# Four attention units on unscaled keys, a fixed order for VectorE's first steps, and eight query tiles

## The chip, the cores and the metric

The program runs on one core of a Trainium2 chip. Its engines are TensorE (PE; PEld is its weight load), VectorE (DVE), ScalarE (ACT), GpSimd (POOL) and SyncE (SP); SP and ACT issue the transfers. The metric is the time of one execution in device microseconds (us), the median of several runs.

## The reference

An attention whose queries see a window of 31 keys and 24 block summaries, then two feed-forward layers. All is float32.

```python
k_sum = k.reshape(B, H, nb, block, D).max(axis=3)      # B 2, H 8, S 768, D 64, block 32
v_sum = v.reshape(B, H, nb, block, D).mean(axis=3)
scores_l = scale * (q @ k.T); mask_l = abs(i - j) < 16
scores_s = scale * (q @ k_sum.T) + log(block)
a = exp(scores_all - max(scores_all)); a = a / (sum(a) + 1e-9)
x = a @ concat([v, v_sum])                             # 1536 tokens x 512
h = x @ w_in;  x = (h * sigmoid(1.702 * h)) @ w_out    # width 2048
out = (sigmoid(x @ w_gate) * (x @ w_val)) @ w_out2     # width 1536
```

## The kernel before, in words

**Attention.** The work is cut into 24 units (b, g, hp): two batches, three groups of four query blocks of 64, four pairs of heads. Units 0 to 11 are batch 0, units 12 to 23 batch 1. A unit needs its query tile (`load_q`, 256 KB) and the keys of its batch and head pair (`load_k`, one tile for three units). `prep_k` takes the block maxima of the keys on VectorE (L670). `w_copy` (L681) lets GpSimd put the windows of keys (128x384) and the maxima (128x128) together into one scaled tile `kx`. `b_pe` writes the mask into PSUM by a matmul with `pick` (L690) and adds four matmuls on `kx` (L692); the scores lie in one of three PSUM tiles `ps_s`. `b_max` (L697) takes the negated row maximum `nm`, `b_exp` (L705) four exponentials, `n_inv` the reciprocal of the sums, `n_mul` (L719, GpSimd) the division; `c_pe` (L725) transposes into `ps_p`, `c_copy` (L730) copies to `pt`, `d_pe` (L744) multiplies with the values, and `d_hi`, `d_lo` (L762, L765) split the result into a high and a low part, xH and xL. `sum_v` (L654) and `sum_lay` (L663, L664) make the block means of the values, `vs`, from the transposed values `vt`.

**Weights.** Each 1 MB piece is fetched by `fetch` (L218) and decoded by `load` in steps: clamp and shift on VectorE (L123), a Prelu on ScalarE (L131), a merge (L137), a cast (L140) and a difference (L142); this gives a high and a low half, so that a product takes three matmuls.

**Feed-forward.** `first` makes ps_h from xH, xL and a piece of w_in (24 matmuls of 512 columns for 512 tokens; the first batch of 512 tokens is made of units 0 to 7); a sigmoid (L501), a product (L485) and a split into gh (ScalarE, L493) and gl (GpSimd, L494) follow; `second` multiplies them with a piece of w_out into ps_o (24 matmuls). Four such steps (`filler`) run among the attention units, the rest behind them.

**Order.** The main loop is written unit by unit, but the order of the compute engines is chosen by a scheduler; SP keeps the order that is written. Every engine works its own list strictly in order, and a matmul that waits holds up all matmuls behind it. A query tile's place comes free when the unit that used it has its scores; before, there are five places. Weight pieces wait for one of two places, key tiles have five.

Of the kernel before, what the change touches and what calls it, by code (L numbers as in the profile page):

```python
# [29 lines left out]
def attention_moe_moe2_kernel(ctx: ExitStack, tc: tile.TileContext, ins: dict, out: bass.AP):  # L30
# [77 lines left out]

    def load(layer, g, i, early):
# [21 lines left out]
        nc.scalar.activation(af, af, AF.Prelu, scale=REBIAS, alpha=-2.0 ** 32)  # L131
# [456 lines left out]
    with tc.manual_schedule(engines={mybir.EngineType.SP}), ExitStack() as es:  # L588
        one = es.enter_context(tc.tile_pool(name="a_one", bufs=1))
        qp = es.enter_context(tc.tile_pool(name="a_q", bufs=5))  # L590
# [9 lines left out]
        pick = one.tile([P, P], BF16, name="pick")  # L600

# [48 lines left out]
        def sum_v(b, hp):  # L650
            if hp == 0:
                vpart[b] = vp.tile([P, HP, W0], F32, tag="vm", name=f"vm{b}")
                nc.vector.memset(vpart[b], 0.0)
            nc.vector.tensor_reduce(  # L654
                out=vpart[b][:, hp, 0:NB], in_=vtl.pop((b, hp)).rearrange("p (n t) -> p n t", t=BLK),
                axis=AX.X, op=ALU.add,
            )

        def sum_lay(b):
            r = vpart.pop(b)  # L660
            ps = ps_a.tile([W0, H * D], F32, tag="x", name="ps_v", bufs=2)
            for hp in range(HP):
                nc.tensor.matmul(ps[:, hp * P:(hp + 1) * P], lhsT=r[:, hp], rhs=ident, start=True, stop=True)  # L663
            nc.scalar.activation(vsum[b][0:W0], ps, AF.Copy, scale=1.0 / BLK)  # L664

        def prep_k(b, hp):
            ks = kp.tile([P, W0], F32, tag="ks", name=f"ks{b}_{hp}")
            nc.vector.memset(ks, 0.0)
            own = kraw[b, hp][:, HALO:HALO + S].rearrange("p (n t) -> p n t", t=BLK)
            nc.vector.tensor_reduce(out=ks[:, 0:NB], in_=own, axis=AX.X, op=ALU.max)  # L670
            kmax[b, hp] = ks

        def w_copy(u):

            b, g, hp = units[u]
            t = kxp.tile([P, G, P], F32, tag="kx", name=f"kx{u}")
            r = kraw[b, hp][:, g * G * QB:g * G * QB + P - W0]
            src = bass.AP(r.tensor, r.offset, [r.ap[0], [QB, G], [1, P - W0]])
            top = kmax[b, hp].unsqueeze(1).to_broadcast([P, G, W0])
            for to, x in ((t[:, :, W0:P], src), (t[:, :, 0:W0], top)):  # L680
                nc.gpsimd.tensor_scalar(out=to, in0=x, scalar1=scale, scalar2=None, op0=ALU.mult)  # L681
            kx[u] = t

        live = {}

        def b_pe(u):
            b, g, hp = units[u]
            t, kt = qbd.pop(u), kx.pop(u)
            ps = ps_a.tile([P, G, P], F32, tag="s", name="ps_s", bufs=3)
            nc.tensor.matmul(ps, lhsT=pick, rhs=mask[:, g:g + G, :], start=True, stop=False)  # L690
            for j in range(G):
                nc.tensor.matmul(ps[:, j, :], lhsT=t[:, j, :], rhs=kt[:, j, :], start=False, stop=j == G - 1)  # L692
            live["s", u] = ps

        def b_max(u):
            nm = sp.tile([P, G], F32, tag="nm", name="nm")
            nc.vector.tensor_reduce(out=nm, in_=live["s", u], axis=AX.X, op=ALU.max, negate=True)  # L697
            live["nm", u] = nm

        def b_exp(u):  # L700
            s, nm = live.pop(("s", u)), live.pop(("nm", u))
            sm = sp.tile([P, G], F32, tag="sm", name="sm")
            e = ep.tile([P, G, P], F32, tag="e", name="e")
            for j in range(G):
                nc.scalar.activation(  # L705
                    e[:, j, :], s[:, j, :], AF.Exp, bias=nm[:, j:j + 1], accum_out=sm[:, j:j + 1]
                )
            live["e", u], live["sum", u] = e, sm

        def n_inv(u):  # L710
            rs = sp.tile([P, G], F32, tag="rs", name="rs")
            nc.vector.tensor_scalar(out=rs, in0=live.pop(("sum", u)), scalar1=EPS, scalar2=None, op0=ALU.add)
            rr = sp.tile([P, G], F32, tag="rr", name="rr")
            nc.vector.reciprocal(out=rr, in_=rs)
# [119 lines left out]
        now = [0]  # L834
        fill = filler()
        for t in range(-1, NU + LD):
# [3 lines left out]
            if u < NU and units[u][1] == 0:  # L840
                prep_k(units[u][0], units[u][2])
            for part, lag in ORDER:
                if 0 <= t - lag < NU:
                    part(t - lag)
            if 0 <= t < NU - 5:
                load_q(t + 5, nc.sync)
            if t == -1:
                sum_v(0, 0)
                sum_v(0, 1)
            if t == 0:  # L850
                sum_v(0, 2)
                sum_v(0, 3)
                sum_lay(0)
                load_v(0, 1)
                put_v(0, 1, nc.scalar)
# [16 lines left out]
            if t >= 1:  # L872
                pull(1 if t < 6 or t > 9 else 2)
# [153 lines left out]
```

## Time and profile before

| | us |
|---|---|
| median of 3 runs | 618.84 (617.81 to 620.34) |
| the profiled execution | 619.4 |
| its span | 617.6 |
| TensorE busy in the span | 603.2 |
| VectorE, ScalarE, GpSimd busy | 465.9, 307.3, 212.7 |

What lies around the span is 1.8 us. A matmul of 128x512 starts every 0.227 us where TensorE runs without a gap, though each is listed with 0.39 us, since they overlap; so a stretch in which TensorE is busy is not always one in which it is full.

### The profile page before, as it was taken

How to read it: one execution, taken by the hardware profiler on the slowest of the kernel's cores; microseconds unless marked ns; L12 is line 12 of the kernel's file. 1: busy time of each engine (PE TensorE's matmuls, PEld its weight loads, DVE VectorE, ACT ScalarE, POOL GpSimd, SP SyncE). 2: the span in 40 equal slices, each digit the busy share in tenths (PEclk: the TensorE clock that was granted, in tenths of full speed). 3: DMA queues.
4: the chain of work that ended last, by engine and by line, in shares of the span. 5: the costliest groups of instructions: out<-in, count | busy, mean ns of one | idle time of the engine just before them, and what ended most of it. 6: DMA issues, size and time to landing. Idle time of an engine off the chain costs nothing.

```text
span 617.6 us, 8819 instructions
## 1 busy us (share of the span) xinstructions
PE 603.2 (98%) x3354; PEld 501.7 (81%) x3354; DVE 465.9 (75%) x684; ACT 307.3 (50%) x614; POOL 212.7 (34%) x168
## 2 busy tenths in 40 slices
PE   7798999999999999999999999999999999999997
PEld 4676777788878888888888898888898898898896
DVE  6699665389998778797769889577969768877434
ACT  4688657556443353435445566635335335444230
POOL 6797585323363423233231232022122021131030
PEclk9899999999999999999999999999999999999999
DMA  9998753034221104040102013321312222100014
GB/s 314 347 313 286 232 137 70 1 121 153 68 69 68 53 17 137 1 137 10 60 0 69 1 40 101 132 69 33 105 69 69 68 69 70 68 1 1 0 49 156
DMA packets 25161, 58.10 MB, mean 94 GB/s; under 512 B 1568, under 2 KB 1824, under 8 KB 25120
## 3 DMA queue, kind: packets, MB, share of 16 engines
q1 hardware_dynamic: 24400, 56.24, 28.0%
q10 hardware_dynamic: 720, 1.31, 0.6%
q8 instruction: 26, 0.43, 0.3%
q14 instruction: 15, 0.12, 0.1%
HBM read 53.08 MB, written 3.15 MB: 91 GB/s over the span
## 4 chain that ended last, share of the span: by engine, by line
PE 81%; DVE 8%; ACT 3%; issue 3%; DMA 2%; POOL 2%; SPq 0%; ACTq 0%; POOLq 0%; DVEq 0%
PE ps_o L474 32%; PE ps_y L178 15%; PE ps_x L178 10%; PE ps_v L178 10%; PE ps_h L474 5%; PE ps_h L178 4%; PE ps_s L692 2%; ACT e L705 1%; PE ps_x L744 1%; DMA raw<-in_moe_w_out 1%; POOL gl L494 1%; DMA vt<-in_vt 1%; PE ps_p L725 1%; DVE da L137 1%; DVE w_0L L142 1%
## 5 line engine op out<-in xcount | busy, mean ns | idle before, releaser
L494 POOL TENSOR_TENSOR gl<-sg,gh 128x512 fp32r<-128x512 f32 x84 | 125.9, 1505 | 362.1 <-ACT gh L493 256.2
L557 DVE TENSOR_TENSOR acc<-ps_o,acc 128x512 f32<-128x512 f32 x143 | 95.9, 683 | 46.7 <-PE ps_o L474 46.6
L474 PE MATMUL ps_o<-gl,w_1H 128*128 128x512 f32 x192 | 75.5, 394 | 0.5 <-POOL gl L494 0.5
L493 ACT CAST gh<-sg 128x512 fp32r<-128x512 f32 x84 | 51.5, 620 | 48.0 <-DVE sg L485 38.6
L474 PE MATMUL ps_o<-gh,w_1H 128*128 128x512 f32 x192 | 74.6, 390 | 0.0
L474 PE MATMUL ps_o<-gh,w_1L 128*128 128x512 f32 x192 | 72.1, 396 | 1.9 <-ACT gh L493 1.7
L474 PE MATMUL ps_o<-w_2L,gh 128*128 128x512 f32 (+1 forms) x146 | 56.6, 388 | 0.0
L474 PE MATMUL ps_o<-w_2H,gh 128*128 128x512 f32 (+1 forms) x146 | 56.2, 386 | 0.0
L474 PE MATMUL ps_o<-w_2H,gl 128*128 128x512 f32 (+1 forms) x146 | 56.2, 389 | 0.1
L137 DVE SCALAR_TENSOR_TENSOR da<-da,db 128x1024 uint32<-128x1024 uint32 x34 | 46.1, 1357 | 5.7 <-ACT da L131 5.1
L131 ACT ACTIVATE da<-da 128x1024 f32<-128x1024 f32 x34 | 36.1, 1061 | 24.7 <-DVE da L123 22.9
L474 PEld LDWEIGHTS ps_o<-gh,w_1L 128*128 128x128 f32 x192 | 35.9, 188 | 9.9 <-ACT gh L493 2.3
L474 PEld LDWEIGHTS ps_o<-gl,w_1H 128*128 128x128 f32 x192 | 36.0, 188 | 8.5 <-POOL gl L494 1.5
L474 PEld LDWEIGHTS ps_o<-gh,w_1H 128*128 128x128 f32 x192 | 36.1, 188 | 7.3
L705 ACT ACTIVATE e<-ps_s,nm 128x128 f32<-128x128 f32 x96 | 34.2, 377 | 9.6 <-DVE nm L697 7.1
L681 POOL TENSOR_SCALAR kx<-k 128x384 f32<-128x384 f32 x24 | 33.3, 1389 | 14.6 <-PE ps_s L692 7.5
L474 PE MATMUL ps_h<-xH,w_0L 128*128 128x512 f32 x96 | 37.7, 401 | 0.0
L474 PE MATMUL ps_h<-xL,w_0H 128*128 128x512 f32 x96 | 37.6, 392 | 0.0
L474 PE MATMUL ps_h<-xH,w_0H 128*128 128x512 f32 x96 | 37.5, 390 | 0.0
L485 DVE TENSOR_TENSOR sg<-ps_h,sg 128x512 f32<-128x512 f32 x32 | 21.7, 682 | 14.1 <-ACT sg L501 11.9
L474 PEld LDWEIGHTS ps_o<-w_2H,gh 128*128 128x128 f32 x146 | 27.4, 188 | 5.8
L474 PEld LDWEIGHTS ps_o<-w_2L,gh 128*128 128x128 f32 x146 | 27.5, 188 | 4.9
(242 smaller groups left out, 1504.5 us busy)
## 6 DMA issues: line engine op xcount, KB each, us to landing
raw<-in_moe_w_out SPq DMA_DIRECT2D x13, 1024.0 KB, 4.9
raw<-in_moe_w_in SPq DMA_DIRECT2D x8, 1024.0 KB, 7.0
raw<-in_moe_w_gate SPq DMA_DIRECT2D x6, 1024.0 KB, 5.1
raw<-in_moe_w_val SPq DMA_DIRECT2D x6, 1024.0 KB, 5.1
q<-in_q SPq DMA_DIRECT2D x20, 256.0 KB, 8.5
vwin<-in_v SPq DMA_DIRECT2D x6, 768.0 KB, 8.6
k<-in_k SPq DMA_DIRECT2D x8, 400.0 KB, 7.2
out<-acc SPq DMA_DIRECT2D x11, 256.0 KB, 2.0
```

The costliest lines, as they stand in the source:

```text
L131: nc.scalar.activation(af, af, AF.Prelu, scale=REBIAS, alpha=-2.0 ** 32)
L137: nc.vector.scalar_tensor_tensor(out=a, in0=a, scalar=3, in1=b, op0=ALU.logical_shift_left, op1=ALU.bitwise_or)
L142: nc.vector.tensor_tensor(out=lo.rearrange(flat), in0=af, in1=hi.rearrange(flat), op=ALU.subtract)
L178: nc.tensor.matmul(ps, lhsT=a[x][:, kk, :], rhs=b[y][:, kk, :], start=start and i == 0, stop=i == n - 1, skip_group_check=True,)
L474: nc.tensor.matmul(ps, lhsT=a, rhs=b, start=i == 0, stop=i == n - 1)
L485: nc.vector.tensor_tensor(out=sg, in0=val, in1=sg, op=ALU.mult)
L493: nc.scalar.copy(gh, sg)
L494: nc.gpsimd.tensor_tensor(out=gl, in0=sg, in1=gh, op=ALU.subtract)
L557: nc.vector.tensor_tensor(out=a[:, m, :], in0=ps, in1=a[:, m, :], op=ALU.add)
L681: nc.gpsimd.tensor_scalar(out=to, in0=x, scalar1=scale, scalar2=None, op0=ALU.mult)
L692: nc.tensor.matmul(ps[:, j, :], lhsT=t[:, j, :], rhs=kt[:, j, :], start=False, stop=j == G - 1)
L705: nc.scalar.activation(e[:, j, :], s[:, j, :], AF.Exp, bias=nm[:, j:j + 1], accum_out=sm[:, j:j + 1])
```

## The change

There are four parts. For units 0 to 3 (`DIRECT`) there is no `kx`: the four window products read the loaded keys (96 columns) and four more the block maxima (32 columns), with a mask scaled by 8 (`pick8`); the scale moves into the exponential, and `nm` gets a multiplication on ScalarE. VectorE's steps of the loop's first rounds (`in_turn`: block maxima, row maxima, sums, means) are tied to one another in the order that is written, with the means spread over rounds 0, 1, 3 and 4 and the last stage of a unit moved by a round. The first weight decode stands behind them. And the query tiles have eight places.

```diff
+    def behind(a, b):
+        tc.add_manual_dep(a.ins, b.ins.name, ... NoSync ..., reason="order")
...
+            elif (layer, g, i) == (1, 0, 0):
+                behind(ins, turn[-1])
...
+        ins = nc.scalar.activation(af, af, AF.Prelu, scale=REBIAS, alpha=-2.0 ** 32)
+        if (layer, g, i) == (1, 0, 0):
+            behind(ins, ahead["exp"])
...
-        qp = es.enter_context(tc.tile_pool(name="a_q", bufs=5))
+        QUERIES = 8
+        qp = es.enter_context(tc.tile_pool(name="a_q", bufs=QUERIES))
...
-            nc.vector.tensor_reduce(out=vpart[b][:, hp, 0:NB], ...)
+            in_turn(nc.vector.tensor_reduce(out=vpart[b][:, hp, 0:NB], ...))
...
+                if b == 0:
+                    behind(ins, live["last"])
...
         def w_copy(u):
+            if u < DIRECT:
+                return
...
+        def in_turn(ins):
+            if now[0] <= ORDERED:
+                if turn:
+                    behind(ins, turn[-1])
+                turn.append(ins)
+        now, ORDERED = [-1], 4
+        DIRECT = HP
...
+            if u < DIRECT:
+                nc.tensor.matmul(ps, lhsT=pick8, rhs=mask[:, g:g + G, :], start=True, stop=False)
+                for j in range(G):
+                    win = kraw[b, hp][:, (g * G + j) * QB:(g * G + j) * QB + P - W0]
+                    nc.tensor.matmul(ps[:, j, W0:P], lhsT=t[:, j, :], rhs=win, start=False, stop=False)
+                for j in range(G):
+                    nc.tensor.matmul(ps[:, j, 0:W0], lhsT=t[:, j, :], rhs=kmax[b, hp], start=False, stop=j == G - 1)
+                return
...
+            if u < DIRECT:
+                nc.scalar.mul(nm, nm, scale)
...
-                    e[:, j, :], s[:, j, :], AF.Exp, bias=nm[:, j:j + 1], accum_out=sm[:, j:j + 1]
+                    e[:, j, :], s[:, j, :], AF.Exp, bias=nm[:, j:j + 1],
+                    scale=scale if u < DIRECT else 1.0, accum_out=sm[:, j:j + 1],
...
         load_v(0, 0)
+        load_q(4, nc.sync)
         sum_load(0, 2)
         sum_load(0, 3)
-        load_q(4, nc.sync)
+        load_q(5, nc.sync)
+        load_q(6, nc.sync)
         fetch()
+        load_q(7, nc.sync)
...
+        nc.vector.tensor_scalar(out=pick8, in0=pick, scalar1=1.0 / scale, scalar2=None, op0=ALU.mult)
...
-            if 0 <= t < NU - 5:
-                load_q(t + 5, nc.sync)
-            if t == -1:
-                sum_v(0, 0)
-                sum_v(0, 1)
+                if part is b_max:
+                    if 0 < t < HP - 1:
+                        prep_k(0, t + 1)
+                    if t in (0, 1, 3, 4):
+                        sum_v(0, {0: 0, 1: 1, 3: 2, 4: 3}[t])
+                    if t == 4:
+                        sum_lay(0)
+                        put_v(0, 1, nc.scalar)
+            if 0 <= t < NU - QUERIES:
+                load_q(t + QUERIES, nc.sync)
             if t == 0:
-                sum_v(0, 2)
-                sum_v(0, 3)
-                sum_lay(0)
...
-            if t >= 1:
-                pull(1 if t < 6 or t > 9 else 2)
+            if t > ORDERED:
+                pull(1 if t > 9 else 2)
```

The first place is SP's list of transfers from the last key tile of batch 0 to the first of batch 1 (`k1_0`; `raw` and `xH1_0_1` are weight pieces of 1 MB, the number behind q is the unit). Before:

```order
L616 DMA q4_150<-in_q 128x512
L218 DMA raw1_0_0_152<-in_moe_w_in 128x4x512
L616 DMA q5_209<-in_q 128x512
...
L218 DMA xH1_0_1_221<-in_moe_w_out 128x2x1024
L616 DMA q6_248<-in_q 128x512
...
L616 DMA q13_584<-in_q 128x512
L218 DMA raw1_1_1_586<-in_moe_w_out 128x2x1024
L647 DMA vt1_1_588<-in_vt 128x768
L609 DMA k1_0_593<-in_k 128x800
```

And the same stretch of SP's list now:

```order
L631 DMA q4_148<-in_q 128x512
...
L631 DMA q6_155<-in_q 128x512
L231 DMA raw1_0_0_157<-in_moe_w_in 128x4x512
L631 DMA q7_159<-in_q 128x512
L631 DMA q8_212<-in_q 128x512
...
L231 DMA xH1_0_1_215<-in_moe_w_out 128x2x1024
...
L631 DMA q16_596<-in_q 128x512
L231 DMA raw1_1_1_598<-in_moe_w_out 128x2x1024
L662 DMA vt1_1_600<-in_vt 128x768
L624 DMA k1_0_605<-in_k 128x800
```

Three more query tiles stand ahead of the first keys of batch 1 (the last one ahead of them is q16, not q13), and of each weight piece two or three more.

The second place is TensorE's list where batch 1 begins (kx12 to kx14 are units 12 to 14; w1_0_0 is the first piece of w_in, w1_0_1 of w_out). Before:

```order
L474 MATMUL ps_h_717<-xH0_321,w1_0_0H_252 128x512
L663 MATMUL ps_v_778<-ident_67,vm1_590 32x128 x2
...
L692 MATMUL ps_s_808<-kx12_733,q12_535 128x128 x4
...
L474 MATMUL ps_o_854<-gh1_0_0_0_793,w1_0_1L_491 128x512
L692 MATMUL ps_s_875<-kx13_805,q13_584 128x128 x4
L474 MATMUL ps_o_862<-gh1_0_0_0_793,w1_0_1L_491 128x512
L725 MATMUL ps_p_949<-ident_67,e_769 128x128 x4
L474 MATMUL ps_o_854<-gl1_0_0_0_794,w1_0_1H_490 128x512
...
L692 MATMUL ps_s_936<-kx14_872,q14_641 128x128 x4
```

The same place in TensorE's list now:

```order
L732 MATMUL ps_s_821<-kx12_743,q12_390 128x128 x4
...
L487 MATMUL ps_h_727<-xH0_378,w1_0_0H_446 128x512
...
L732 MATMUL ps_s_884<-kx13_818,q13_440 128x128 x4
...
L487 MATMUL ps_o_863<-gh1_0_0_0_806,w1_0_1L_553 128x512
L487 MATMUL ps_o_871<-gh1_0_0_0_806,w1_0_1L_553 128x512
L732 MATMUL ps_s_943<-kx14_881,q14_499 128x128 x4
...
L487 MATMUL ps_o_863<-gl1_0_0_0_807,w1_0_1H_552 128x512
```

Unit 12 now stands ahead of the last four matmuls of ps_h instead of behind them, unit 13 ahead of the first ps_o instead of behind it, and unit 14 ahead of the products on gl.

The third place is ScalarE's list between the sigmoids of that step and the two casts gh. Before:

```order
L501 ACTIVATE sg_788<-ps_h_704 128x512
L501 ACTIVATE sg_790<-ps_h_717 128x512
L140 CAST w1_1_1H_849<-da_847 128x1024
L762 CAST xH1_765<-ps_x_828 128x256
L493 CAST gh1_0_0_0_793<-sg_788 128x512
L705 ACT_TABLE_LOAD
L705 ACTIVATE e_839,sm_838<-ps_s_808,nm_814 128x128 x4
L493 CAST gh1_0_0_1_798<-sg_790 128x512
```

And the same place of ScalarE's list now:

```order
L514 ACTIVATE sg_801<-ps_h_714 128x512
L514 ACTIVATE sg_803<-ps_h_727 128x512
L142 ACTIVATE da_1053<-da_1053 128x1024
L747 ACT_TABLE_LOAD
L747 ACTIVATE e_852,sm_851<-ps_s_821,nm_827 128x128 x4
L805 CAST xH1_775<-ps_x_841 128x256
L681 ACTIVATE vs1_114<-ps_v_788 32x512
L506 CAST gh1_0_0_0_806<-sg_801 128x512
L506 CAST gh1_0_0_1_811<-sg_803 128x512
```

The first cast gh moved behind the Prelu of a weight piece, the table load, a unit's exponentials, a cast xH and the copy vs; the cast of the weight piece moved behind both gh.

## Rows read from the trace of the kernel before

**Rows 1.** Busy time of each engine by stage; columns: stretch, length, engines, clock, DMA

```profile
core 0: us, PE busy (x) PEld busy (x) DVE busy (x) ACT busy (x) POOL busy (x), PEclk, DMA share, GB/s
0.00:30.00 30.00, 22.92 (x180) 16.15 (x180) 19.77 (x51) 16.65 (x57) 21.07 (x29) 0.94 0.98 329
30.00:48.00 18.00, 16.93 (x172) 13.54 (x167) 16.99 (x33) 15.12 (x57) 16.67 (x14) 1.00 1.04 325
48.00:58.00 10.00, 8.24 (x88) 6.26 (x88) 10.00 (x19) 9.21 (x22) 7.37 (x7) 1.00 1.05 349
58.00:64.00 6.00, 5.27 (x42) 3.42 (x40) 6.00 (x9) 4.54 (x19) 4.65 (x4) 1.00 0.17 44
64.00:104.00 40.00, 39.94 (x315) 32.56 (x316) 23.76 (x52) 25.76 (x85) 27.95 (x30) 1.00 0.59 169
104.00:617.60 513.60, 509.91 (x2570) 429.80 (x2568) 389.39 (x525) 236.00 (x380) 135.00 (x87) 1.00 0.19 62
```

**Rows 2.** TensorE's waits from 60 us to the end: total, times, longest

```profile
PE ps_x L744 <- DVE pt L730: 0.6, 1, 0.6
PE ps_o L474 <- POOL gl L494: 0.5, 1, 0.5
```

**Rows 3.** VectorE from the first keys to the first weight decode

```profile
4.35:23.02 18.67, 12.15 (x20) 0.91 1.05 353
```

**Rows 4.** TensorE in order of time: start, duration, instruction, idle before and releaser

```profile
6.04 2.08 PE L692 MATMUL ps_s<-kx,q 128*128 128x128 f32 x8 [0.83 <-POOL kx L681]
51.81 0.40 PE L474 MATMUL ps_h<-xH,w_0H 128*128 128x512 f32 x1
52.92 1.05 PE L692 MATMUL ps_s<-kx,q 128*128 128x128 f32 x8
57.23 0.50 PE L474 MATMUL ps_o<-gh,w_1L 128*128 128x512 f32 x1 [1.71 <-ACT gh L493]
```

**Rows 5.** TensorE's busy time and granted clock in two stretches

```profile
14.30:17.70 3.40, 1.57 (x12) 0.99 1.02 380
17.70:21.10 3.40, 3.40 (x17) 0.50 1.06 364
```

**Rows 6.** GpSimd in order of time

```profile
4.32 1.17 POOL L681 TENSOR_SCALAR kx<-k 128x384 f32<-128x384 f32 x1 [0.60 <-DMA k<-in_k]
48.49 1.48 POOL L681 TENSOR_SCALAR kx<-k 128x384 f32<-128x384 f32 x1 [1.28 <-DMA k<-in_k]
51.79 0.53 POOL L681 TENSOR_SCALAR kx<-ks 128x128 f32<-128x128 f32 x1 [1.82 <-DVE rr L714]
57.26 1.27 POOL L494 TENSOR_TENSOR gl<-sg,gh 128x512 fp32r<-128x512 f32 x1 [0.32 <-ACT gh L493]
```

**Rows 7.** DMA issues up to 120 us: KB each, us to landing

```profile
q<-in_q SPq DMA_DIRECT2D x20, 256.0 KB, 8.5
k<-in_k SPq DMA_DIRECT2D x8, 400.0 KB, 7.2
```

**Rows 8.** ScalarE in order of time

```profile
51.23 1.08 ACT L131 ACTIVATE da<-da 128x1024 f32<-128x1024 f32 x1
54.37 1.08 ACT L501 ACTIVATE sg<-ps_h 128x512 f32<-128x512 f32 x2
56.27 0.39 ACT L762 CAST xH<-ps_x 128x256 fp32r<-128x256 f32 x1
56.54 0.64 ACT L493 CAST gh<-sg 128x512 fp32r<-128x512 f32 x1
57.19 1.28 ACT L705 ACT_TABLE_LOAD   x1
58.49 0.37 ACT L705 ACTIVATE e<-ps_s,nm 128x128 f32<-128x128 f32 x1
59.87 0.63 ACT L493 CAST gh<-sg 128x512 fp32r<-128x512 f32 x1
```

**Rows 9.** TensorE's busy time before and after its first product of the second kind

```profile
57.23:65.63 8.40, 7.67 (x69) 1.00 0.40 83
54.55:57.23 2.68, 0.97 (x21) 1.00 1.08 276
```

More of the change, by code (lines that the diff above doesn't have):

```diff
@@ L107, in attention_moe_moe2_kernel @@
     ps_h = ctx.enter_context(tc.tile_pool(name="ps_h", bufs=2, space=PSUM))
+    turn, ahead = [], {}
+    def behind(a, b):
+        tc.add_manual_dep(
+            a.ins, b.ins.name,
+            mybir.DependencyInfo(mybir.DependencyClass.NoSync, mybir.DependencyReason.DATA), reason="order",
+        )
     def load(layer, g, i, early):
@@ L600, in attention_moe_moe2_kernel @@
         pick = one.tile([P, P], BF16, name="pick")
+        pick8 = one.tile([P, P], BF16, name="pick8")
         units = [(b, g, hp) for b in range(B) for g in range(NG) for hp in range(HP)]
@@ L669, in prep_k @@
             own = kraw[b, hp][:, HALO:HALO + S].rearrange("p (n t) -> p n t", t=BLK)
-            nc.vector.tensor_reduce(out=ks[:, 0:NB], in_=own, axis=AX.X, op=ALU.max)
+            in_turn(nc.vector.tensor_reduce(out=ks[:, 0:NB], in_=own, axis=AX.X, op=ALU.max))
             kmax[b, hp] = ks
         def w_copy(u):
+            if u < DIRECT:
+                return
             b, g, hp = units[u]
@@ L704, in b_exp @@
             for j in range(G):
-                nc.scalar.activation(
-                    e[:, j, :], s[:, j, :], AF.Exp, bias=nm[:, j:j + 1], accum_out=sm[:, j:j + 1]
+                ahead["exp"] = nc.scalar.activation(
+                    e[:, j, :], s[:, j, :], AF.Exp, bias=nm[:, j:j + 1],
+                    scale=scale if u < DIRECT else 1.0, accum_out=sm[:, j:j + 1],
                 )
@@ L711, in n_inv @@
             rs = sp.tile([P, G], F32, tag="rs", name="rs")
-            nc.vector.tensor_scalar(out=rs, in0=live.pop(("sum", u)), scalar1=EPS, scalar2=None, op0=ALU.add)
+            in_turn(nc.vector.tensor_scalar(out=rs, in0=live.pop(("sum", u)), scalar1=EPS, scalar2=None, op0=ALU.add))
             rr = sp.tile([P, G], F32, tag="rr", name="rr")
-            nc.vector.reciprocal(out=rr, in_=rs)
+            in_turn(nc.vector.reciprocal(out=rr, in_=rs))
             live["rr", u] = rr
@@ L816, in attention_moe_moe2_kernel @@
         )
+        ahead["kx"] = ins
         nc.vector.memset(pick, 0.0)
@@ L832, in filler @@
                 yield from second(layer, g, blk, False, True)
-        now = [0]
         fill = filler()
@@ L839, in attention_moe_moe2_kernel @@
             u = t + 2
-            if u < NU and units[u][1] == 0:
+            if t < 0:
+                prep_k(0, 1)
+            elif HP <= u < NU and units[u][1] == 0:
                 prep_k(units[u][0], units[u][2])
             for part, lag in ORDER:
-                if 0 <= t - lag < NU:
+                late = lag == LD and part not in (c_pe, c_copy)
+                if late and t == LD + 1:
+                    part(0)
+                if 0 <= t - lag < NU and not (late and t == LD):
                     part(t - lag)
-            if 0 <= t < NU - 5:
-                load_q(t + 5, nc.sync)
-            if t == -1:
-                sum_v(0, 0)
-                sum_v(0, 1)
+                if part is b_max:
[8 more added lines that the diff above has]
+                load_q(t + QUERIES, nc.sync)
             if t == 0:
-                sum_v(0, 2)
-                sum_v(0, 3)
-                sum_lay(0)
                 load_v(0, 1)
-                put_v(0, 1, nc.scalar)
                 fetch()
```

22 lines of the change are left out of this document (12 added, 10 removed).

## The prediction

> **What bounds the kernel now.** I read the busy times by stage first. In the 513.6 us behind 104 us TensorE is busy for 509.91, and between 64 and 104 us for 39.94 of 40 [rows 1]. The view of waits says the same: from 60 us to the end TensorE waited twice, 1.1 us together [rows 2]. So from 64 us on the time is TensorE's work, which the change leaves as it is, and a gain can only come from TensorE reaching a given piece of work earlier, ahead of 64 us. Its listed idle time there is 7.08 us up to 30 us, 1.07 up to 48, 1.76 up to 58 and 0.73 up to 64, 10.6 us in all [rows 1], of which the first 4.3 us pass before the first keys are there [rows 6].
>
> The same table shows what fills that time. DMA's share is 0.98 up to 30 us, 1.04 to 48 and 1.05 to 58, and 0.17 from 58 to 64 [rows 1]: the transfers run without a hole until batch 1's data is in, at 325 to 349 GB/s. VectorE has room at the start (12.15 us of the 18.67 from the first keys to the first weight decode, 6.52 idle [rows 3]) but none from 48 to 64 us (10.00 of 10, 6.00 of 6). Then I read the engines in order of time around the largest hole of TensorE that is not at the start: 54.55 to 57.23 us, of which only 0.97 is busy [rows 9]. It ends when ScalarE has cast the first gh [rows 4].
>
> **The change part by part.** My sum goes by three meetings: the start, the first keys of batch 1, and the first product on gh.
>
> *The start.* Four units lose GpSimd's two copies, 1.17 and 0.53 us each [rows 6], 6.8 us of its 21.07 in the first 30 [rows 1]; with them go some 1.7 us between a key tile's landing and its scores. Against it each of the four units has 8 matmuls instead of 4, so 16 passes instead of 8. Eight passes of 128 columns took 2.08 us for unit 0 and 1.05 for unit 12 [rows 4]. The columns stay the same, so one bound is no cost; the other is that each short pass takes as long as a long one, 2.08 us more per unit, 8.3 in all. Eight of the sixteen passes keep most of their columns, and I take +1 us per unit. It lies in TensorE's 7.08 idle us. [...] The four multiplications of nm on ScalarE are not in the trace: more than nothing, at most an exponential's 0.37 us each [rows 8]. `pick8`, one 128x128 step on VectorE, costs at most GpSimd's 0.53 for that shape [rows 6], while VectorE waits for keys. The fixed order of VectorE's steps takes out of its 6.52 idle us what it can: the lead of units 3 to 8 is between nothing and 6.5 us, and I take 3, the middle, because the order also puts unit 3's keys in front of unit 2's maxima on TensorE.
>
> *Query tiles and batch 1.* Three more query tiles stand ahead of batch 1's first keys on SP, 3 x 256 KB [rows 7], 0.79 MB. At the 325 GB/s of 30 to 48 us [rows 1] that is 2.4 us. The queue is full there, so a transfer put in front pushes the rest: bounds are 0 (if those tiles land in time that is lost now) and 3.2 us (at 245 GB/s, three quarters of that rate); I take 2.4. Before, the keys landed at 48.49 us, where GpSimd's wait for them ended [rows 6], and unit 12's scores began at 52.92 [rows 4], 4.4 us later, with VectorE full. Now they land at 50.9. With the lead, the path from there is one copy of 1.17 us, one of 0.53 [rows 6] and some 0.1 of handing over: 52.7. So the lead of 3 us is down to 0.2 here. This is the step on which the forecast rests.
>
> *The first product on gh.* The last four ps_h matmuls, which ended at 52.21 (51.81 + 0.40 [rows 4]), now stand behind unit 12: 52.7 + 1.05 + 4 x 0.227 = 54.6. The two sigmoids, 1.08 us [rows 8], then end at 55.7; before they ended at 55.45. Behind them ScalarE now has a Prelu (1.08), a table load (1.28), four exponentials (58.49 to 59.87, 1.38), a cast xH (0.27 from its start to the next), the copy vs (not in the rows, at most the 0.63 of gh) and the cast gh, 0.64 [rows 8]: 55.7 + 5.3 = 61.0 instead of 57.2. The wait is new, and it is TensorE's whole list that stands behind it: the ps_o, unit 14 and the transposes. What pays for it is work already done: from 57.23 to 65.63 us TensorE was busy 7.67 us [rows 9], and of that unit 13 (1.05 as unit 12 [rows 4]), and about 1.4 us of a mask, the sums' products, a transpose and a product of an attention unit now stand ahead of the gh. 61.0 + 7.67 - 2.45 = 66.2, against 65.63. GpSimd's gl, 1.27 us each [rows 6], at 62.3 and 63.5, come in time for the rest. The sum: 0.6 us later at the place from which TensorE runs full.
>
> *Behind it.* From unit 23's scores on, all engines have the same lists as before. The vs that frees SP's next transfers comes some 2 us earlier, so unit 15's keys do too; I count nothing for it.
>
> The profiled execution took 619.4 us, 1.8 more than its span and 0.56 more than the median. 619.4 + 0.6 is 620.0; against the median, 619.4. Because the lead of 3 us may be 6.5, which takes up the last waits, while the price of the gh is near its upper end (xH and vs need not both come in full behind the exponentials), I halve the loss to 0.3 and forecast 619.1: no change.
>
> **Rivals.** *The lead is carried through.* If the key tiles of batch 1 land as early as before, unit 12 starts at 48.5 + 1.8 = 50.3, the sigmoids end at 53.3, gh comes at 58.6 and the place of 66.2 at 63.8, 1.8 us ahead of before; if the table load falls into a wait, its 1.28 goes too: 3.1. That is 615.7. For it: VectorE's idle time is at the start, and a faster start makes SP's requests earlier. Against it: DMA's share of 1.04 leaves no place for earlier requests. By the clock rows TensorE ran at 0.50 (1.2 GHz) from 17.7 to 21.1 us, after a stretch in which it was busy 1.57 of 3.40 us [rows 5]; a list that waits less would keep 2.4 GHz there and win up to half of these 3.4 us. [...]
>
> *Batch 1 comes late, slower.* If unit 12 keeps the 4.4 us behind its keys, it starts at 55.3, the ps_h end at 57.2, gh comes at 63.6 and the place of 66.2 at 68.8, 3.2 us later than before: 622.0. It decides once unit 12's scores start after 54 us. For it: VectorE has no idle time from 48 to 64 us [rows 1], and two of batch 1's sums of values and two key maxima now stand ahead of the products that gh waits for. Against it: with the lead VectorE has less left by then.
>
> *The change does not do what it says.* If sixteen passes at 1.2 GHz take 4.16 us (twice unit 0's 2.08 [rows 4]), units 0 to 3 have their scores no earlier and the lead is nil. VectorE is then as late at 48 us as before, and the outcome lies between the forecast and the slower rival, about 620.5.
>
> **How the numbers follow.** The forecast, with the lead eaten by the transfers, 0.40; the lead carried, 0.38; batch 1 late, 0.15; a nil lead, 0.07. Half a per cent, 3.1 us, is about what a measurement can tell from no change, so faster is below 615.75 and slower above 621.9. The carried lead is centred on that lower edge and can reach 612.5 with all of the 6.5 us; some two thirds of it count as faster, 0.25, and an eighth of the forecast, 0.05: 0.30. The late batch, half of it above 621.9 by its own errors, gives slower 0.08, a third of the nil lead 0.02, and a holdup that I have not seen in the new lists 0.05: 0.15. The forecast's own range is 616.5 to 621; with the others 613.5 to 622.5.
>
> **What would show it.** Right: unit 4's row maximum (VectorE) done earlier than before; the first keys of batch 1 land at 50 to 52 us; unit 12's scores within 2 us behind them; a wait of TensorE for gh of some 3 us that ends near 61; no idle TensorE behind 66. Wrong: batch 1's keys at 48.5 or earlier, with TensorE full from 60 us on; then the carried lead is right. If the first maxima are no earlier, the start failed; if TensorE waits behind 70 us, a list I took as full was not.

## The result and the profile after

The changed kernel takes 627.26 us (median of 4 runs, 625.10 to 629.12) against 618.91 before: 1.0132 times as long, 95% interval 1.0090 to 1.0174. The forecast was 619.1 us and no change, the range ended at 622.5. It is slower, and by more than any of the cases had.

The profiled execution took 625.1 us, its span 623.3, 5.7 us more than before. It is the fastest of the four; the 2.2 us up to the median are in no trace. First the stages, with the columns of [rows 1]:

```profile
0.00:30.00 30.00, 27.41 (x166) 22.77 (x168) 17.44 (x49) 13.88 (x52) 14.66 (x22) 1.00 0.98 330
30.00:48.00 18.00, 14.99 (x210) 12.35 (x205) 15.90 (x34) 16.06 (x55) 13.67 (x12) 1.00 1.02 316
48.00:58.00 10.00, 9.53 (x82) 6.96 (x80) 9.69 (x17) 9.10 (x27) 9.35 (x8) 1.00 0.98 337
58.00:64.00 6.00, 3.89 (x35) 3.02 (x34) 6.00 (x11) 5.83 (x15) 3.68 (x5) 0.89 0.34 75
64.00:104.00 40.00, 40.00 (x310) 32.84 (x309) 26.53 (x51) 25.48 (x86) 28.68 (x29) 0.97 0.56 171
104.00:623.30 519.30, 513.08 (x2602) 432.44 (x2600) 390.73 (x529) 240.59 (x388) 137.09 (x88) 1.00 0.19 61
```

Add up TensorE's column and those of [rows 1]: 608.9 us busy and 14.4 idle, against 603.2 and 14.4. The idle time is the same. It only lies elsewhere: 4.5 us less of it in the first 30 us, 1.9 more up to 48, and 2.5 more behind 104. The 5.7 us are time in which TensorE works: 4.5 us more in the first 30 us, 3.2 more behind 104, and 2.0 less in between. The order of time on TensorE there (start, duration, instruction; an entry of x8 is eight passes: the trace lists each fp32 product of the scores twice) says on what:

```profile
4.62 2.02 PE L726 MATMUL ps_s<-k,q 128*128 128x96 f32 x8 [0.18 <-DMA q<-in_q]
...
7.29 1.75 PE L728 MATMUL ps_s<-ks,q 128*128 128x32 f32 x8
...
16.14 1.81 PE L728 MATMUL ps_s<-ks,q 128*128 128x32 f32 x8
...
18.17 1.91 PE L732 MATMUL ps_s<-kx,q 128*128 128x128 f32 x8
...
20.58 1.12 PE L768 MATMUL ps_p<-ident,e 128*128 128x128 f32 x4
...
22.00 1.08 PE L728 MATMUL ps_s<-ks,q 128*128 128x32 f32 x8
...
24.02 0.60 PE L768 MATMUL ps_p<-ident,e 128*128 128x128 f32 x4
```

Eight passes of 32 columns take 1.75 to 1.81 us, eight of 96 take 2.02, eight of 128 take 1.91. Between 32 and 128 columns they hardly differ. A direct unit holds TensorE for 3.8 us where a unit with copies held it for 2.08 [rows 4]; added up over the trace, the passes of units 0 to 3 take 14.3 us, and before they took 7.7. Unit 0's scores begin at 4.62 instead of 6.04, 1.4 us earlier, and end at 9.04 instead of 8.12.

Two rows show the clock: the four transposes of `ps_p` take 1.12 us at 20.58 and 0.60 at 24.02. The trace gives the granted clock as a share of full: half clock here is 0.50, which the recorded texts call 1.2 GHz, and full clock is 1.00, their 2.4 GHz; no run shows a frequency. The clock's first event in this trace is a rise at 21.7 us; before, it was at 14.3. (The column PEclk reads 1.00 ahead of the first event, also where the durations are those of half clock, like the 1.12 us above.) Stretches of TensorE, columns as in [rows 5]:

```profile
4.60:21.70 17.10, 17.08 (x75) 1.00 1.04 364
...
58.00:62.70 4.70, 2.59 (x30) 1.00 0.24 57
62.70:66.10 3.40, 3.40 (x27) 0.50 0.87 231
```

TensorE works without a hole from 4.6 to 21.7 us (17.08 of 17.10 us busy), all of it with the durations of half clock. The fall to 0.50 that came at 17.7 us before [rows 5] now comes at 62.7, behind 4.70 us in which TensorE was busy for 2.59.

VectorE waits for these scores (row maxima of units 0 to 4, the first decode, and the seventh and ninth row maximum, of units 6 and 8, with the idle time before them):

```profile
9.08 0.69 DVE L737 TENSOR_REDUCE nm<-ps_s 128x4 f32<-128x512 f32 x1 [1.81 <-PE ps_s L728]
...
12.49 0.69 DVE L737 TENSOR_REDUCE nm<-ps_s 128x4 f32<-128x512 f32 x1 [1.86 <-PE ps_s L728]
...
17.99 0.69 DVE L737 TENSOR_REDUCE nm<-ps_s 128x4 f32<-128x512 f32 x1 [2.79 <-PE ps_s L728]
...
23.12 0.69 DVE L737 TENSOR_REDUCE nm<-ps_s 128x4 f32<-128x512 f32 x1 [3.29 <-PE ps_s L728]
...
25.06 0.66 DVE L737 TENSOR_REDUCE nm<-ps_s 128x4 f32<-128x512 f32 x1
...
27.63 0.66 DVE L132 TENSOR_SCALAR da<-raw 128x1024 f32<-128x1024 f32 x1
...
29.26 0.68 DVE L737 TENSOR_REDUCE nm<-ps_s 128x4 f32<-128x512 f32 x1
...
37.89 0.68 DVE L737 TENSOR_REDUCE nm<-ps_s 128x4 f32<-128x512 f32 x1
```

Before (units 2, 3 with 4, 6 and 8):

```profile
14.61 0.69 DVE L697 TENSOR_REDUCE nm<-ps_s 128x4 f32<-128x512 f32 x1 [1.20 <-PE ps_s L692]
...
21.68 1.29 DVE L697 TENSOR_REDUCE nm<-ps_s 128x4 f32<-128x512 f32 x2 [2.82 <-PE ps_s L692]
...
32.92 0.65 DVE L697 TENSOR_REDUCE nm<-ps_s 128x4 f32<-128x512 f32 x1
...
36.57 0.65 DVE L697 TENSOR_REDUCE nm<-ps_s 128x4 f32<-128x512 f32 x1
```

For the scores of the first four units VectorE waits 9.8 us; before, it was 4.0. The maximum of unit 2 is done 3.4 us later than before and that of unit 4 2.8 later, that of unit 6 3.6 us earlier, and that of unit 8 1.4 later again. The first decode is at 27.63 us; before, it was at 23.02, the end of the stretch in [rows 3]. It was behind unit 4's maximum then and is behind unit 5's now, where the change puts it. Then batch 1 and the first gh, which answer to [rows 6] and [rows 4], on GpSimd and on TensorE:

```profile
51.21 1.68 POOL L700 TENSOR_SCALAR kx<-k 128x384 f32<-128x384 f32 x1 [0.65 <-DMA k<-in_k]
```

```profile
54.37 1.16 PE L732 MATMUL ps_s<-kx,q 128*128 128x128 f32 x8 [0.47 <-POOL kx L700]
...
62.35 0.93 PE L487 MATMUL ps_o<-gh,w_1L 128*128 128x512 f32 x2 [0.84 <-ACT gh L506]
...
105.74 1.05 PE L732 MATMUL ps_s<-kx,q 128*128 128x128 f32 x8
```

Unit 12's scores come at 54.37 (before 52.92), the first product on gh at 62.35 (57.23), and the last unit's scores, of unit 23, at 105.74; in the trace of before these stood at 103.08. Up to here 2.7 us are lost, behind it 3.0. TensorE's waits from 60 us on, against [rows 2]:

```profile
PE ps_x L787 <- DVE pt L773: 1.5, 1, 1.5
PE ps_s L730 <- ACT e L747: 1.3, 1, 1.3
PE ps_o L487 <- POOL gl L507: 1.1, 2, 0.7
PE ps_o L487 <- ACT gh L506: 0.8, 1, 0.8
PE ps_o L487 <- DVE sg L498: 0.4, 1, 0.4
```

The waits for pt, gl and sg, 3.0 us, lie behind unit 23's scores; before, the 0.5 for gl did.

### The profile page after: what moved, and what is told of

Read it like the earlier page. It is cut to its first block, busy times and chain, and to the rows that moved or that the text cites. A ratio compares the mean times of both kernels' runs of the same rounds, so it can differ in the third digit from the quotient of the medians.

```text
span 623.3 us, 8888 instructions
## 1 busy us (share of the span) xinstructions
PE 608.9 (98%) x3386; PEld 510.4 (82%) x3386; DVE 466.3 (75%) x685; ACT 310.9 (50%) x620; POOL 207.1 (33%) x160
## 4 chain that ended last, share of the span: by engine, by line
PE 79%; DMA 6%; issue 5%; ACT 3%; DVE 3%; POOL 3%; ACTq 0%; POOLq 0%; SPq 0%
PE ps_o L487 33%; PE ps_y L191 15%; PE ps_x L191 10%; PE ps_v L191 10%; PE ps_h L487 5%; PE ps_h L191 3%; DMA xH<-in_moe_w_out 2%; POOL gl L507 2%; DMA vt<-in_vt 2%; DMA vt_early<-in_vt 1%; PE ps_s L732 1%; PE ps_x L787 1%; DMA q<-in_q 1%; PE ps_p L768 1%; ACT e L747 1%
## 5 line engine op out<-in xcount | busy, mean ns | idle before, releaser
L487 PEld LDWEIGHTS ps_o<-gh,w_1L 128*128 128x128 f32 x192 | 36.0, 188 | 10.2 <-ACT gh L506 2.5
L762 POOL TENSOR_TENSOR e<-e,rr 128x512 f32<-128x512 f32 x24 | 28.3, 1183 | 29.1 <-DVE rr L757 19.9
L487 PEld LDWEIGHTS ps_o<-w_2H,gh 128*128 128x128 f32 x146 | 27.4, 188 | 5.7
```

The source lines that it names most:

```text
L487: nc.tensor.matmul(ps, lhsT=a, rhs=b, start=i == 0, stop=i == n - 1)
L762: nc.gpsimd.tensor_tensor(out=e, in0=e, in1=rr.unsqueeze(2).to_broadcast([P, G, P]), op=ALU.mult)
```

## The experiments

Names with a_ and d1_ are edits of the changed kernel, with b_ of the one before. All ratios are to the kernel before, run beside each on the same chip. For each kernel the table has TensorE's busy and idle time in its profile, and how much of the busy time was at half clock (ahead of the clock's first rise, and in its falls to 0.50). A profile is of one execution; it is up to 2.3 us off the median (changed 2.2 below, b_warm8 2.3 above).

| kernel | us | ratio, 95% interval | busy | idle | at half clock |
|---|---|---|---|---|---|
| before | 618.9 | 1 | 603.2 | 14.4 | 14.0 |
| changed | 627.3 | 1.0132 [1.0090, 1.0174] | 608.9 | 14.4 | 23.0 |
| b_direct | 630.3 | 1.0177 [1.0163, 1.0191] | 612.0 | 16.5 | 28.9 |
| b_q8 | 625.1 | 1.0098 [1.0080, 1.0116] | 606.0 | 18.8 | 18.8 |
| a_order_only | 623.2 | 1.0066 [1.0052, 1.0080] | 603.1 | 18.2 | 13.5 |
| a_no_direct | 624.2 | 1.0081 [1.0067, 1.0095] | 602.7 | 18.9 | 13.2 |
| a_q5 | 633.5 | 1.0236 [1.0222, 1.0250] | 613.7 | 17.8 | 33.0 |
| a_no_turn | 626.8 | 1.0125 [1.0111, 1.0138] | 610.2 | 15.1 | 26.6 |
| a_direct1 | 619.6 | 1.0007 [0.9996, 1.0018] | 603.5 | 14.0 | 15.0 |
| a_direct1_q6 | 621.1 | 1.0033 [1.0023, 1.0044] | 603.8 | 15.5 | 15.3 |
| a_direct1_q5 | 623.6 | 1.0075 [1.0056, 1.0095] | 605.3 | 16.2 | 17.1 |
| a_warm16 | 628.2 | 1.0142 [1.0124, 1.0159] | 606.2 | 18.7 | 8.4 |
| a_warm8 | 627.4 | 1.0138 [1.0123, 1.0153] | 609.0 | 16.7 | 19.0 |
| b_warm8 | 621.1 | 1.0034 [1.0020, 1.0049] | 604.3 | 17.3 | 13.0 |
| b_warm12 | 620.4 | 1.0020 [1.0009, 1.0030] | 604.4 | 14.7 | 11.4 |
| d1_warm8 | 620.3 | 1.0019 [1.0010, 1.0028] | 604.4 | 14.1 | 13.3 |
| a_late | 630.2 | 1.0185 [1.0161, 1.0208] | 612.3 | 15.9 | 29.5 |
| a_qlate | 635.7 | 1.0274 [1.0258, 1.0290] | 613.6 | 20.9 | 31.0 |
| a_warm8_qlate | 631.5 | 1.0204 [1.0183, 1.0224] | 607.2 | 22.6 | 10.6 |

Most of the added busy time goes with the last column. At half clock TensorE's work takes about twice as long (the transposes above, 1.12 against 0.60 us), so half of that column is an estimate of what the lower clock adds. From before to changed it is 4.5 of the 5.7 us of busy time, for b_direct 7.5 of 8.8, for a_q5 9.5 of 10.5: with four direct units most of the time that TensorE is busy longer is the lower clock, and about 1 us is left. In the kernel before itself a single fall costs less than half of its 3.4 us: of its executions beside these runs 38 have a mean granted clock of 0.997, that of one fall, and a median of 619.2 us, and 23 have 1.000, that of none, and 618.4.

**Which part costs: the change taken apart.** One part undone or one part alone, in six kernels. The direct units undone:

```diff
-        DIRECT = HP
+        DIRECT = 0
-                    if 0 < t < HP - 1:
-                        prep_k(0, t + 1)
+                    if 0 <= t < HP - 2:
+                        prep_k(0, t + 2)
```

> The changed kernel with all units on GpSimd's copies again (no scores straight from the keys); key maxima 2 and 3 stand one step earlier in VectorE's order, since the copies need them; eight query tiles and the other orders stay. Theory 1, passes: what costs is TensorE's own work. Each of the four direct units holds TensorE for about 3.8 us (8 passes of 96 columns 2.0, 8 of 32 columns 1.8) where 8 passes of 128 took 2.08 at the same clock, about 7 us in all, and idle time in the whole span is the same 14.4 us before and after. Then this kernel loses most of the 8 us: 618 to 621 us, TensorE busy about 602 to 604 us. Theory 2, query tiles: the keys of batch 1 land 2.7 us later because three more tiles stand ahead of them; then this stays at 624 to 627. Theory 3, order: VectorE's fixed order and ScalarE's gh behind the exponentials make the hole at 60 us and the waits behind 104 us; then this stays at 623 to 627 as well, with the hole at 60 us still there.

Measured 624.2 us: 3.1 us of the 8.3 go, not 7. TensorE's busy time falls as theory 1 had it, by 6.2 us to 602.7, but 4.5 us of idle time come in its place, at waits like these (the longest waits of TensorE, columns as in [rows 2], over the whole span):

```profile
PE ps_s L732 <- POOL kx L700: 4.5, 3, 3.0
PE ps_s L730 <- ACT e L747: 2.4, 4, 1.0
PE ps_s L732 <- DMA q<-in_q: 1.9, 1, 1.9
```

The 3.0 are unit 12's copy, whose keys land at 51.96 us although the direct units are gone.

The direct units alone, five query tiles, no order: in `b_pe`, `b_max`, `b_exp` and `w_copy` of the kernel before

```diff
+            if u < DIRECT:
+                return
...
+            if u < DIRECT:
+                nc.tensor.matmul(ps, lhsT=pick8, ...)
...
```

> The kernel before with the direct scores of units 0 to 3 alone (scaled mask row, maxima scaled on ScalarE); five query tiles and no fixed order. Theory 1, passes: slower by most of the loss, 623 to 627 us, TensorE busy 607 to 610. Theory 2, query tiles: as before, 618 to 620. Theory 3, order: as before or a little faster, 616 to 620, since GpSimd's copies and their 1.7 us per unit are gone.

Measured 630.3, more than any theory had: 11.3 us, of them 8.8 busy. Four units of 1.7 us more are 6.8; here the clock is also at 0.50 from 66.3 to 73.1 us, a fall within a stretch, 65 to 67 us, in which TensorE does nothing.

Five query tiles, with the loads of q5 to q7 left out at the start and that of q4 moved back to its old place:

```diff
-        QUERIES = 8
+        QUERIES = 5
```

> The changed kernel with five query tiles and the load order of the kernel before. Theory 1, passes: 625 to 628 us, no change. Theory 2, query tiles: 622 to 624.5, with batch 1's first keys issued at about 38 us instead of 41 and unit 12's scores about 2 us earlier. Theory 3, order: 625 to 628.

No fixed order of VectorE, and with it no tie of the first decode:

```diff
-                if turn:
-                    behind(ins, turn[-1])
-                turn.append(ins)
+                pass
```

> The changed kernel without the fixed order of VectorE's first steps and of the first decode (the scheduler places them); direct scores, eight query tiles and the orders of the sums' products, copies and Prelu stay. Theory 1, passes: 624 to 628 us, since TensorE's passes are all still there. Theory 2, query tiles: 624 to 628. Theory 3, order: 619 to 622, with the first decode at 23 to 25 us instead of 27.6 and without the hole at 60 to 62 us.

633.5 and 626.8. Five tiles beside four direct units are 6.2 us worse than eight, the reverse of theory 2; without the order nothing changes, as theory 1 said, although the first decode then starts at 22.08 us, earlier than before. The two remaining parts alone, eight tiles in the kernel before (with the first loads in their new order), then the order, which is the changed kernel with `DIRECT = 0` and `QUERIES = 5` as above:

```diff
-        qp = es.enter_context(tc.tile_pool(name="a_q", bufs=5))
+        qp = es.enter_context(tc.tile_pool(name="a_q", bufs=QUERIES))
```

> The kernel before with eight query tiles and the changed kernel's order of the first loads, and nothing else. Theory Q-late, as predicted: three more tiles ahead of batch 1's keys, 2.4 us later: 619 to 622 us, unit 12's copies beginning at 50.5 to 51.5 us instead of 48.5. Theory Q-free: the tiles take waits out of SP's queue (five tiles alone cost 6 us beside the direct scores), so 615 to 618.5 us, keys no later than 49.

> The changed kernel without direct scores and with five query tiles and the load order of before: VectorE's fixed order, the sums' products behind the direct units' place, the copies behind the mask and the first Prelu behind the exponentials are all that is left. Theory order-costs: the 5 us that stay when only the direct scores go (624.2) are the order's, so 622 to 626 us. Theory sum-of-parts: the order is worth nothing alone and the 5 us are the query tiles': 618 to 620 us.

625.1 and 623.2 us. So each of the three parts (the decode counted with the order) is slower alone: 11.3, 5.8 and 4.0 us; their sum would be 21, together they cost 8.3. They are not additive. In the three kernels without direct units the loss is mostly idle time (18.2 to 18.9 us against 14.4), with four of them it is mostly busy time.

**How many direct units.** The edit has the key maxima moved as in a_no_direct.

```diff
-        DIRECT = HP
+        DIRECT = 1
```

> The changed kernel with one direct unit instead of four: 8 more passes instead of 32. Theory passes: the loss over the kernel without direct units (624.2 us) is a quarter of that of four (3 us of time, 6 us of TensorE's busy time): 624 to 626 us, TensorE busy some 604 to 605 us, and TensorE's passes at full rate from about 12 to 16 us on instead of 22. Theory start: TensorE waits 1 us for unit 0's first copy, which one direct unit takes away: 622 to 624 us.

619.6 us, the same as before, and 4.6 us better than none: neither theory had that. With this list the loss comes with the other three: from one direct unit to four the time grows by 7.7 us, TensorE's busy time by 5.4 and its time at half clock by 8.0. The orders and the eight tiles are all still there in this kernel, and cost nothing with this list. With `QUERIES = 5` and `QUERIES = 6`:

> The changed kernel with one direct unit and five query tiles in the load order of before. With eight tiles and one direct unit (619.6 us) batch 1's first keys land at 51.9 us against 48.5 before, and TensorE has a hole of 3.3 us from 48 to 58 and a fall of its clock. Theory query tiles: the keys land near 49 us, the hole and the fall go, 615 to 618 us. Theory tail: ScalarE's list has ten table loads instead of eight, two of them among the last units, 2.6 us: 620 to 624 us.

> As the one with one direct unit and five query tiles, with six tiles. Theory query tiles: keys at about 49.5 us, 615.5 to 618.5 us. Theory tail: ten table loads here too, 620 to 624 us.

623.6 and 621.1. GpSimd's copies of batch 1's first keys do begin at 49.5 and 49.9 us instead of 51.9, as theory query tiles had it, and the time is longer: an earlier landing of these keys is not what decides. Both times are in the range of theory tail, and both kernels have its ten table loads; a_late below tests that theory.

**What a pass costs, and the clock.** Five streams of idle products ahead of everything:

```diff
+        for n, cols in ((64, 32), (64, 96), (64, 128), (64, 32), (64, 96)):
+            ps = ps_h.tile([P, TB], F32, tag="h", name=f"ps_{cols}")
+            for i in range(n):
+                nc.tensor.matmul(ps[:, 0:cols], lhsT=zero, rhs=zero[:, 0:cols], ...)
```

> The kernel before with five streams of 64 idle fp32 products (two passes each) on a zero tile ahead of everything, one behind the other on TensorE: 32 columns, 96, 128, 32, 96. The output is not touched; the start is some 100 us later, so its time says nothing of the change. Theory passes: a pass takes nearly the same whatever its columns, 0.22 to 0.26 us at 1.2 GHz and about 0.13 at 2.4 GHz: each stream of 128 passes takes 28 to 33 us slow, 16 to 18 fast. Theory columns: a pass of 32 columns takes half of one of 128 or less. Theory clock: the granted clock stays at 1.2 GHz through the first stream of 32 columns, rises in a wider one and falls or not in the second narrow one; if it rises within the first stream, narrow passes do not hold it down.

Groups of passes by shape in stretches of this run (36 to 44, 45 to 56, 58 to 66 and 68 to 88 us): the count, busy us, mean ns of one.

```profile
L789 PE MATMUL ps<-zero 128*128 128x96 f32 x74 | 8.4, 275 | 0.0
...
L789 PE MATMUL ps<-zero 128*128 128x128 f32 x82 | 9.3, 275 | 0.0
...
L789 PE MATMUL ps<-zero 128*128 128x32 f32 x44 | 5.0, 274 | 0.0
...
L789 PE MATMUL ps<-zero 128*128 128x32 f32 x76 | 16.4, 401 | 0.0
L789 PE MATMUL ps<-zero 128*128 128x96 f32 x19 | 4.3, 426 | 0.0
```

8.4 / 74, 9.3 / 82 and 5.0 / 44 are 0.114, 0.113 and 0.114 us: at full clock a pass costs the same with 96, 128 or 32 columns. At half clock it is 16.4 / 76 = 0.216 with 32 and 4.3 / 19 = 0.226 with 96, about twice as much. That a pass costs the same with 32, 96 or 128 columns is shown, though theory passes had its price at full clock a little too high (0.13); theory columns is out. The stretches of the clock (columns as in [rows 5]):

```profile
58.00:66.00 8.00, 8.00 (x75) 1.00 0.00 0
68.00:88.00 20.00, 20.00 (x95) 0.50 0.00 1
```

TensorE is busy in every moment of both. The whole first stream of 32 columns runs at half clock by its durations (27.4 us for 128 passes, 0.214 each), and the clock rises about 5 us into the one of 96 (12 passes are listed from 32 to 34 us, 21 from 36 to 38); it falls to 0.50 at 66 us, 5 us into the second narrow stream, and rises at 90, in the last wide one. These are the rows that theory clock expected, and a fall besides. The prediction has a list that waits less keep the clock [rows 5]; here it fell without a wait, with TensorE busy for 8.00 us of 8.00 up to 66 us.

**Whether the clock is the lever.** More idle products of 128x512 at the start:

```diff
-        for _ in range(4):
+        for _ in range(16):
```

> The changed kernel with sixteen instead of four idle products on the zero tile (128x512, bf16, about 0.43 us each at 1.2 GHz); most of the twelve more stand between the direct units' passes, so they add full-width work there. They cost 2.6 to 5.2 us of TensorE at the start. Theory clock: the direct passes leave TensorE at 1.2 GHz until 22 us; beside full-width products the clock rises earlier (by 10 to 15 us), the later direct units take about 2 us instead of 3.8, and the time is 624 to 628 us. Theory passes alone: the clock rises at 20 us or later all the same, and the time is 628 to 632 us.

The clock rose at 6.2 us, theory clock was right on that; the time, 628.2, is 0.2 past the end of its range. 14.6 us less at half clock are offset by 4.3 us more of idle time and by the twelve added products. With `range(8)`:

> The changed kernel with eight instead of four idle products (128x512, bf16) ahead of the first scores. Theory clock: the clock rises before the direct units or within the first two (5 to 12 us instead of 21.7), TensorE is busy at 1.2 GHz for 8 to 15 us in all instead of 23, and the time falls by 3 to 6 us to 621 to 624 us, unless idle time grows by as much. Theory passes: the clock rises at about 20 us all the same, or its rise changes nothing: 626 to 629 us.

TensorE in order of time, then its two stretches:

```profile
4.87 1.03 PE L726 MATMUL ps_s<-k,q 128*128 128x96 f32 x8
...
6.16 0.97 PE L728 MATMUL ps_s<-ks,q 128*128 128x32 f32 x8
...
15.25 1.75 PE L728 MATMUL ps_s<-ks,q 128*128 128x32 f32 x8
```

```profile
4.70:11.60 6.90, 5.83 (x50) 1.00 1.03 398
11.60:21.80 10.20, 10.20 (x47) 0.50 1.05 341
```

Unit 0 takes 2.00 us instead of 3.8, about twice a copied unit's 1.05 [rows 4] at full clock. Then, among the direct units, the clock falls to 0.50 at 11.6 and stays down for 10.2 us with TensorE busy throughout. So the time at half clock is 19.0 us, not the 8 to 15 expected, and the time is 627.4, unchanged: what is won at the start is not carried. ScalarE stands there for 6.14 us ahead of its copy `vwin<-vs` and the exponentials behind it (ScalarE in order of time):

```profile
31.74 0.72 ACTq L648 DMA_DIRECT2D vwin<-vs  x1
32.51 0.37 ACT L747 ACTIVATE e<-ps_s,nm 128x128 f32<-128x128 f32 x1 [6.14 <-DMA xH<-in_moe_w_out]
```

In the kernel before that copy went out at 22.80, in the changed one at 30.02.

The same in the kernel before, with `range(8)` and `range(12)`, and in the one with a single direct unit:

> The kernel before with eight instead of four idle products ahead of the first scores. Theory clock: it rises at 6 to 10 us instead of 14.3, and if it then stays, busy time at 1.2 GHz falls from 14 us to 6 or 8: 615 to 617 us, faster than before. If TensorE's waits up to 20 us let it fall once as before, 617 to 619. Theory passes: no change, 618 to 620 us.

> The kernel before with twelve idle products. Theory clock: as with eight, with 0.9 us more of idle work at full clock in front: 615 to 618 us. Theory passes: 619 to 622 us, since the added products push unit 0's scores back by up to 3 us.

> The kernel with one direct unit and eight query tiles (619.6 us) with eight instead of four idle products. Theory clock: the rise comes at 6 to 10 us instead of 14.8: 615 to 617.5 us. Theory passes: 618.5 to 621 us.

621.1, 620.4 and 620.3: the first two are 1.9 and 1.1 us slower than without the added products, the third 0.7, which the intervals do not tell apart. The clock rose at 4.4 to 5.8 us in all three and fell two or three times behind that, so TensorE worked at half clock for about as long as without them (13.0, 11.4 and 13.3 us against 14.0 and 15.0). The time goes with these falls: of b_warm8's executions five with a mean granted clock of 0.997 took 619.4 to 620.0 us, four with 0.992 or less 622.1 to 623.4. So the added products have failed as a lever on the time. Only a_warm16 took much of the time at half clock away; what the clock alone is worth stays open.

**Whether the transfers are the second floor.** The three added tiles behind the second values and the second weight:

```diff
-        load_q(5, nc.sync)
-        load_q(6, nc.sync)
...
             if t == 0:
                 load_v(0, 1)
                 fetch()
+                for x in (5, 6, 7):
+                    load_q(x, nc.sync)
```

> The changed kernel with eight query tiles, the three added ones behind the load of the second values and the second weight. Theory transfers: ScalarE's copy vwin<-vs goes out at 23 to 26 us instead of 30.0 and waits for nothing; since the direct passes at 1.2 GHz last till 22 us all the same, the time falls by 0 to 3 us, 624 to 627.5. Theory clock alone: the transfers do not matter beside the passes, 626 to 628.5 us.

And the same with `range(8)` for the idle products:

> The same with eight idle products, so that the first direct units run at 2.4 GHz. Theory transfers: with both floors lower the start is worth something at last: the copy vwin<-vs at 23 to 25 us, no hole of TensorE from 28 to 33 us, 620 to 624 us. Theory clock alone: as the raised clock without it, 626 to 629 us. If the time stays though the copy goes out early and the hole is gone, what the start wins is lost again behind it, in holes of the new lists.

635.7 and 631.5, worse than all expectations. The copy went out at 32.70 and 28.48, not at 23 to 26, in the second case within 8.66 idle us of ScalarE for which the trace names nothing that it waited for. So neither edit brought about what the theory starts from, an early copy; that ScalarE's wait in a_warm8 is a second floor was neither shown nor refuted.

**The tail.** The two sigmoids of one step set side by side behind the exponentials recorded before them:

```diff
+            if (layer, g, blk) == (1, 0, 1):
+                behind(gates[-2], ahead["exp"])
```

> The changed kernel with one order added: the two sigmoids of the step (1,0,1), which now stand on either side of an attention unit's exponentials, come behind the exponentials recorded before them and side by side. The lists of all engines are the same up to about 97 us; behind it ScalarE has one change of tables there and back less (2 x 1.28 us). Theory tail: the 2.6 us that TensorE idles between 104 and 130 us (23.43 busy of 26; before 25.98) come from these table loads in front of the last units' exponentials: 104 to 130 us at 25 or more busy, and 624 to 626 us, 1.5 to 3 less than the changed kernel's 627.3. Theory start: the tail only passes on what was lost ahead of it, and the time stays within 1 us of 627.3.

630.2. Two table loads less, and TensorE is busy for 22.54 us from 104 to 130, not more than 25. Its waits in that stretch:

```profile
PE ps_x L789 <- DVE pt L775: 2.7, 1, 2.7
PE ps_o L487 <- ACT gh L506: 0.8, 1, 0.8
```

The wait for pt grew from 1.5 to 2.7, and a fall of the clock followed it (0.50 from 111.0 to 117.8 us). Without the two table loads the waits are still there; theory tail is not borne out.

None of these kernels beats the one before; the one with a single direct unit equals it.

## Why the prediction was wrong

*The start* is the step that failed. "The lead of units 3 to 8 is between nothing and 6.5 us, and I take 3", with "+1 us per unit" that "lies in TensorE's 7.08 idle us". Each direct unit cost 1.7 us more than a copied one, near the upper bound I had written down (2.08), because a pass costs a pass, with 32, 96 or 128 columns (0.113 to 0.114 us at full clock in b_passes), and TensorE was at half clock there; at full clock the +1 would have been right (2.00 us in a_warm8 against the 1.05 of a copied unit [rows 4]). The four took 6.6 us more in all, and they did not fit into the idle time. Of the 7.08 us 5.2 lay behind the first keys at 4.32, and 1.9 ahead of them, not the 4.3 that I gave (TensorE of the kernel before, columns as in [rows 5]):

```profile
4.32:30.00 25.68, 20.49 (x176) 0.93 1.04 351
```

TensorE became the bound of the start, at half clock until 21.7 us instead of 14.3, and VectorE waited for it. Its row maxima of units 0 to 4 were done 0.1 to 3.4 us later than before, so the first were no earlier, which I had named as the sign of a failed start. Those of units 5 to 7 came 0.9 to 3.6 us earlier, so a lead like the 3 us that I took was there for three units only; units 8 to 11, the last ahead of batch 1, were 0.8 to 3.3 us late again. My interval for the lead ended at nothing; it left out that the covering engine could turn into the bound.

*Query tiles and batch 1.* The keys landed at 51.2 us; 50.9 was forecast. The number is right, and eight tiles alone do that (b_q8, 51.7). But so do four direct units with five tiles (b_direct 52.3, a_q5 52.2), a delay that I did not have, so the agreement is in part luck. Unit 12's scores came 3.2 us behind the keys, not within 2. That this landing decides is not borne out: a_direct1 has it at 51.9 and loses nothing, and five and six tiles beside one direct unit have it earlier and are slower.

*The first product on gh.* Forecast 61.0, measured 62.35. The new wait was there, but as 1.3 us for the exponentials that now stand ahead and 0.8 for gh, not 3 for gh. Unit 12's scores at 54.37 are past the 54 us from which my rival of the late batch decides. It gave 3.2 us of loss; at unit 23's scores 2.7 were measured. Up to there that rival was nearer than the forecast. It held a chance of 0.15, since I thought VectorE would have the lead to work off.

*The change does not do what it says.* Its condition came true, units of 3.8 us against my 4.16, but I priced it as a nil lead and 620.5.

*Behind it.* "All engines have the same lists as before" from unit 23's scores on was wrong for ScalarE, whose two sigmoids of one step stand apart there, and it says nothing of when the lists are entered. 3.0 us were lost behind 105.74, 2.5 of them in TensorE's waits. "No idle TensorE behind 66" was on my list of what would show me right; TensorE was idle for 6.2 us behind 104, and for 3.7 before. None of my cases had a price for this stretch.

*What stays open.* That the direct units add 5.4 to 8.8 us of TensorE's busy time, most of it at half clock, is shown by three pairs (none and four, one and four, before and alone). Why the time then moves by 3.1, 7.7 or 11.3 us is not: every edit has the scheduler write new lists up to 105 us, and idle time comes and goes by 4 us with them. Why the clock stays down longer beside direct units, and what makes the tail wait, is not shown either.

## What to carry to other kernels

Before splitting a matmul to save a copy, count passes and not columns (32, 96 and 128 columns cost 0.113 to 0.114 us a pass here at full clock), and price them at the clock that the trace shows at that place; one split unit was free here, four were not. When an edit lets a scheduler rewrite the lists, run each part alone and each part undone before believing a sum of terms: here three parts that cost 11, 6 and 4 us cost 8 together. And give the stretch behind the last place you have worked out a price of its own.

## What the runs showed of the hardware that I had not expected

A pass of an fp32 product took 0.113 to 0.114 us at full clock with 32, 96 or 128 columns, and at half clock 0.216 with 32 and 0.226 with 96 (b_passes). In the same run the first 128 passes of 32 columns, 27.4 us without a gap, took 0.214 us each, the price of half clock, and the granted clock fell to 0.50 at 66 us while TensorE was busy in every moment. Among the direct units of a_warm8 it fell to 0.50 at 11.6 us, behind 6.90 us with 5.83 busy, and stayed down for 10.2 us without a gap in TensorE's work.
